# A new hand-made issue order for the last four fifths of an attention and gated convolution kernel

## The chip, the cores and the metric

The program runs on one core of one Trainium2 chip. The metric is device time in microseconds (us) of one execution; lower is better. The core's engines are TensorE (PE, with its weight loads shown as PEld), VectorE (DVE), ScalarE (ACT), GpSimd (POOL) and SyncE (SP). SP computes nothing here: it is the queue from which every DMA is issued, one after the other.

## What is computed

Packed attention and then a gated feed-forward block, for 8 batch elements, 8 heads, 576 tokens, head size 64:

```python
p_packed = sm_attn(p, k, v)           # 32 packed queries attend to the 576 tokens
out = sm_attn(q, p_packed, p_packed)  # the 576 tokens attend to the 32 packed rows
x = out, heads side by side           # (8, 576, 512)
h = np.maximum(x @ w_in, 0.0)         # 512 -> 1024
conv_out[s] = sum over k of conv_w[k] * h[s + k - 1]     # three taps along the tokens
gate = 1.0 / (1.0 + np.exp(-conv_out))
return (h * gate) @ w_out             # 1024 -> 512
```

## The kernel before

The work is cut into 271 streams, each a Python generator of steps. A step is one or a few instructions on one engine. The table `ORDER` is a string of two-digit numbers in base 36; each number names a stream, and the program issues that stream's next step. So the table fixes, for each engine, the order in which its instructions are issued, and each engine takes them strictly in that order. Semaphores between the engines are put in by the framework where data or a buffer demands it; the order alone decides how long somebody stands at one. All 1525 steps are in the table.

```python
flow.run([int(ORDER[i : i + 2], 36) for i in range(0, len(ORDER), 2)])
```

`Flow` also carries planned times, but they decide one thing only: how many idle matmuls are put in on PE (`fill`) until the first output matmul has been issued. That happens before step 331.

The streams that matter here, with g a group of four heads of one batch element (16 groups), b a batch element, j one of 8 blocks of 128 hidden features, m one of 36 blocks of 128 output rows:

- **load_kq(g, k or q)**, L405 from group 4 on: four DMAs issued by SP. There are three buffers (`kq`) for all keys and queries, so a load waits until an earlier `head_transpose` has read its buffer.
- **head_transpose(g, k or q)**, L417: one DVE transposition, which gives that buffer back.
- **attention(g)**: scores on PE (L450), row maximum on DVE (L495), exponential on ACT (L499). From group 10 on the 128 x 576 result is transposed by DVE (L507 and L509) and its blocks are put in place by **16 DMAs on SP** (L515, the "moves" below) into the one buffer `a1T`; before group 10 PE does this. Then comes the product P times V on PE (L535, step 5 of the stream), which reads all of `a1T`. A scaling on ACT, a transposition on PE, the second scores on PE (L450), and a softmax of nine DVE and two ACT steps (L559 to L589) follow.
- **packed_weight(b, half)**: PE (L609), a copy on ACT, and the low part on DVE (L632).
- **ffn1(b, j)**: 12 matmuls (L661), then ACT and DVE in turn up to L689.
- **ffn2(m)**: a cast on ACT (L700), a difference on DVE (L703), eight PE steps of three matmuls each (L752), a copy on ACT (L760) and the store, a DMA on SP (L762).

The moves as they stand in the code:

```python
yield Step("SP", 1100, take=["a1T"], give=["ad"], parts=4 * HG)
...
for q in range(4):
    for h in range(HG):
        nc.sync.dma_start(
            out=a1T[32 * q : 32 * q + 32, h].rearrange("r s n -> r (s n)"),
            in_=moved[32 * h : 32 * h + 32, q].rearrange("r s n -> r (s n)"),
        )
```

Of the kernel before, what the change touches and what calls it, by code (L numbers as in the profile page):

```python
# [23 lines left out]
    "060u3r3z0h3w0e3u0u0e463z0q0u0m0e0w060e460v0n0e46170p0m3z0e0m0e0m0u463x3x0u3z0m0m3x143v0m170v3v0m3v48494a48494849"  # L24
    "400t4a48470t47493z0x0m174a48494910474a490u4a12483z474a4b120u0u0t0m48124b1f4b0u120t124c0m4a13184c1f1f4c414b1a1341"
    "1a4c0m4b414d1a4d4b4g1242124c4b1a0u4g4g0u121a4e41126e4d4c4g4341411n4e430u6e0u0m4c0m1b6e4f1n0u6e1c1g1i4h1544431n0m"
    "4f430u1d1i1b4d1a1i430u1a4f450y1k3o290m0u454h4d1a4d1a6e0u1i1i4h45454e6e1i454f0u4f4d0u430u4f4e4f4i4h4e454j11124i4e"
    "4e1j1j4j7e4i1v127e4k1i6f6e4i1o6e1v6e6e4k4k1v234j1q4i6f6e4k4i1q6f6f7f6f1q4i1l1i4l1q6f7f6f6f1r4j6g6g4j121r4k1i1q16"
    "1s1w3p286e1219236f4l6f4l4k232b7g1q1y121a4k6f1q1q1q121y124m7g4l124l4m2b2b4m4j6f1e1m1t124m1a6g4l6g6g6g6g6g6g4m6h6h"
    "4l4m7h1a4m4j1h6g6g1y4n4n7h4n2j4n1a4o4o4p4o4p4p4o4n4p126h6h6h1y4p4o4n4n6h6h6h6h6h1y4p124o206g1a4p6h4o6i1i1y4q4r4q"  # L30
    "1a126i1a1i1z241a4q6i1z1y6j6i6i6i6i6i6i1y6i6i1a1p1a266j1q1y1a4r2j6j6j6j6j2626266j1i2j6k6j6j6j1u1q1i2g6h2r1i1a2c1q"
    "4r1i4s1x1q264t2e6k4s6j4s2r4t4s6k6k6k4t1q2r2e2z4t1i4t4s2e6l22211i6j6i2o6k6k6k4u6k6k4t4s27276l4t1i1q4u4v4s2k1i2e1q"
    "6k4v4v4v4u4w6l261y4w4v4w4u4w1y4v2m26502650261q2f4u6l6l4w2z6l6l6l6l4u4v1i1q4u4w6l1i501q4w6m2z6l4x4y4x6m4x4z4y4x2m"
    "4x4y4z1q4x4z2m374y1q4y4z4x4z4y4y4z4z6n2w6k2p2e6m6m6m6m6m6m6m6m5253542s2m1y2f6m5252536l6m2e5125266n522e54542u2e6n"
    "6n6n6n6n6n6n6n6o5126545253262e52531y521y54556o546n531y2n261y2n555551546o376o6o6o6o6o6o6o536p1y556p2i2h302u53566o"
    "5556266p6p576p6p342m6p5637556p6p6p1y6q2u6n57562626562a6o566q551y575726562u58576p6q596q6q6q6q586q6q6q58582d2e592m"
    "323f592v5957582v5958575859596r1y5a6q2e2m266r1y5b2e266r6r6r6r6r6r3f322l5a26265a5b6s3f6p2q322e6s332x2u6r6r5c5d2m3c"
    "6r2e5c5d2m5c5d6s322e6s385c332e2m2u2m6t6t5d5b3a2u5d2m2e2u5d2u3a6s6s6s3a5d5e5e356q5c6s6s6s2m2y6r322e6s5c5f6t6t2m5e"
    "5f6s3b5c5f3b2m5e2m5f6t6t6t6t6t2t5e2m5f5e5e2e5f6t5f3a3g6t2e6u6u5g5g5g5h5i5h5i5i5k5k32322u3i6v5g2m5g5k5g5h2e5g5i5h"
    "6u6u6u6u6u6u326u6u5j6u5j5j2m6v313i2m5i5i322u3i2m366t3a5j5h5j5j6v6v5h6v6v6v6v6v6v325l2u5j5h5i3a32325l6w5m5n6v6w5m"  # L40
    "5m3a6u6w6x5n2u5m5m5m2u6w6w6w6w6w3a3a6w5l6x5n39326w6w6y5o6x6x6x6v3e3d6x6x6x6x6x3i6y3j32325n5o5o5o5o5o5m2u6x5p6z5o"
    "2u2u32325n6w2u2u5n5p5p5n5p3i6y5p5q6y6y5q5q5q5p5r6y6y6y6y5q5q2u5p5r5r5q6x6z2u5s6y6y6y5t5s5s3j5r325r5s5s6z6z6z6z6z"
    "6z6z6z5r5t5t5t5s5r5t5s5t5t703a3i5u325v326z3a707070707070705v3a323a713a3h5u3i70703i703i3a5u715w7271726z705w3i5w5w"
    "3i5x5x5x3i3a3i5x5x5x5w3a3a5w71717171717171713i3a3i5y3i5v3a5y5y735y72727272725y5y5y72725w3a725z5x3i71605z733i3i5z"
    "72726173737373737373735z5z3i615z606061743i5z60606062746073637461616263637374636361626262646564747474747474646361"
    "6262637575666674667667757575757575757566676567666667756667657467766768697676767676767676777577696968686868687669"
    "696a7868786a69696a6a6a6a77776a6b6c77776d6b6b6c6c6b6b6b6b777777776c6d6d6c6d6d776c6c786d6d797878787878787876787877"
    "7979797979797979797a797a7b7b7a7a7a7a7a7a7a7a7b7b7b7b7b7b7b7b7c7a7a7c7d7b7b797d7c7c7c7c7c7c7c7c7d7c7c7d7d7d7d7d7d"
    "7d7d7d7i7i7d7d7d7d7d7d7d7d"
)  # L50


# [768 lines left out]
```

## Time and profile before

| | |
|---|---|
| median of 3 runs | 405.0 us (404.56 to 406.21) |
| the profiled execution, its own time | 402.9 us |
| its span, first to last instruction | 401.1 us |
| PE busy | 394.1 us (98%) |
| PE weight loads busy | 316.2 us (79%) |
| DVE busy | 341.4 us (85%) |
| ACT busy | 276.3 us (69%) |
| DMA traffic | 49.19 MB, 123 GB/s on average |

A matmul's record overlaps the next one's, so the distance between starts is what a matmul costs, not its record's length. Step 331 of the table is the ffn1 step that lies near 75 us: all that PE, DVE, ACT and SP do up to there is the same in both tables.

### The profile page before, as it was taken

Reading aid. Unit: us, or ns where it says so; the run is one execution under the profiler, and the core shown is the slowest. Engines: PE = TensorE matmul, PEld = TensorE weight load, DVE = VectorE, ACT = ScalarE, POOL = GpSimd, SP = SyncE. Lnnn points to the kernel's source line nnn. Section 1 sums busy time; section 2 is a strip of 40 time slices with the busy share of each in tenths; the row PEclk is TensorE's granted clock in tenths of the full one; section 3 lists DMA queues with packets and bytes.
Section 4 is the critical chain, followed back from the end, with each engine's and each line's share of the span. In section 5 each row is a group of like instructions: output and inputs, shape, how many; then the busy total and the mean of one; then the engine's idle time right before and its main releaser. Section 6 shows DMA issues by size and latency. Waiting matters only on the chain.

```text
span 401.1 us, 8199 instructions
## 1 busy us (share of the span) xinstructions
PE 394.1 (98%) x3297; PEld 316.2 (79%) x3297; DVE 341.4 (85%) x494; ACT 276.3 (69%) x475; POOL 0.9 (0%) x12
## 2 busy tenths in 40 slices
PE   7999999999999999999999999999999999999996
PEld 6667666777968878888877877889678878898886
DVE  0699999999999999999999999999889976786220
ACT  4899999976856787766674685766766576576221
POOL 0000000000000000000000000000000000000000
PEclk9999999999999999999999999999999999999999
DMA  8989998997728771554446551621010000000121
GB/s 289 399 305 274 248 257 231 214 185 132 159 48 155 174 156 49 94 125 94 105 107 136 121 99 58 136 88 37 28 55 26 28 26 28 26 26 2 52 81 52
DMA packets 140378, 49.19 MB, mean 123 GB/s; under 512 B 121244, under 2 KB 132788, under 8 KB 140340
## 3 DMA queue, kind: packets, MB, share of 16 engines
q1 hardware_dynamic: 140340, 48.67, 48.2%
q8 instruction: 26, 0.43, 0.4%
q14 instruction: 12, 0.10, 0.1%
HBM read 37.25 MB, written 9.44 MB: 116 GB/s over the span
## 4 chain that ended last, share of the span: by engine, by line
PE 78%; ACT 7%; SPq 7%; DMA 4%; DVE 1%; issue 1%; ACTq 0%
PE fo L752 41%; PE big L661 20%; PE sm L752 5%; PE big L450 4%; SPq L515 3%; SPq L405 3%; PE big L609 3%; PE sm L535 2%; PE big L434 2%; DMA v<-in_v_dram 1%; DMA out_dram<-o 1%; PE big L525 1%; DMA hgt<-in_k_dram 1%; DMA a1T<-stage 1%; ACT hgt L265 1%
## 5 line engine op out<-in xcount | busy, mean ns | idle before, releaser
L752 PE MATMUL fo<-wo_hi,xhi 128*128 128x512 f32 (+1 forms) x264 | 106.1, 402 | 0.0
L752 PE MATMUL fo<-wo_hi,xlo 128*128 128x512 f32 (+1 forms) x264 | 103.3, 391 | 0.0
L752 PE MATMUL fo<-wo_lo,xhi 128*128 128x512 f32 (+1 forms) x264 | 103.0, 390 | 0.0
L687 ACT ACTIVATE hgt<-hgt 128x576 f32<-128x576 f32 x64 | 43.9, 693 | 26.2 <-DVE hgt L683 25.7
L752 PEld LDWEIGHTS fo<-wo_hi,xhi 128*128 128x128 f32 x264 | 49.9, 189 | 14.3 <-issue 2.4
L679 DVE SCALAR_TENSOR_TENSOR hgt<-hbuf,cw,hgt 128x576 f32<-128x576 f32 x64 | 51.4, 808 | 10.3 <-ACT hgt L677 9.8
L703 DVE TENSOR_TENSOR xlo<-hgt,xhi 128x1024 fp32r<-128x1024 f32 (+1 forms) x44 | 44.5, 1017 | 18.4 <-ACT xhi L700 18.2
L752 PEld LDWEIGHTS fo<-wo_hi,xlo 128*128 128x128 f32 x264 | 49.6, 188 | 12.0
L673 ACT ACTIVATE hbuf<-big 128x576 f32<-128x576 f32 x64 | 41.7, 655 | 23.3 <-PE big L661 22.8
L752 PEld LDWEIGHTS fo<-wo_lo,xhi 128*128 128x128 f32 x264 | 49.6, 188 | 9.2
L661 PE MATMUL big<-a2hi,ghi 128*128 128x288 f32 x256 | 55.5, 298 | 0.0
L661 PE MATMUL big<-a2hi,glo 128*128 128x288 f32 x256 | 54.3, 294 | 0.0
L661 PE MATMUL big<-a2lo,ghi 128*128 128x288 f32 x256 | 54.2, 293 | 0.0
L683 DVE SCALAR_TENSOR_TENSOR hgt<-hbuf,cw,hgt 128x576 f32<-128x576 f32 x64 | 51.0, 804 | 0.7
L677 ACT ACTIVATE hgt<-hbuf,cw 128x576 f32<-128x576 f32 x64 | 49.7, 783 | 1.2
L689 DVE SCALAR_TENSOR_TENSOR hgt<-hgt,hbuf 128x576 f32<-128x576 f32 x64 | 47.1, 749 | 3.3 <-ACT hgt L687 2.8
L700 ACT CAST xhi<-hgt 128x1024 fp32r<-128x1024 f32 (+1 forms) x44 | 39.0, 890 | 12.7 <-DVE hgt L689 4.7
L661 PEld LDWEIGHTS big<-a2hi,ghi 128*128 128x128 f32 x256 | 42.4, 188 | 5.6 <-issue 0.9
L661 PEld LDWEIGHTS big<-a2lo,ghi 128*128 128x128 f32 x256 | 40.9, 188 | 0.0
L661 PEld LDWEIGHTS big<-a2hi,glo 128*128 128x128 f32 x256 | 40.8, 188 | 0.0
L760 ACT COPY o<-fo 128x512 f32<-128x512 f32 (+1 forms) x33 | 19.0, 577 | 28.0 <-PE fo L752 27.5
L495 DVE TENSOR_REDUCE nm<-big 128x1 f32<-128x576 f32 x16 | 11.8, 740 | 11.4 <-PE big L450 11.4
(91 smaller groups left out, 505.4 us busy)
## 6 DMA issues: line engine op xcount, KB each, us to landing
out_dram<-o SPq DMA_DIRECT2D x35, 256.0 KB, 2.2
v<-in_v_dram SPq DMA_DIRECT2D x16, 512.0 KB, 5.1
k<-in_k_dram SPq DMA_DIRECT2D x48, 144.0 KB, 3.3
q<-in_q_dram SPq DMA_DIRECT2D x48, 144.0 KB, 3.3
hgt<-in_moe_w_in_dram SPq DMA_DIRECT2D x3, 1024.0 KB, 8.8
hgt<-in_moe_w_out_dram SPq DMA_DIRECT2D x3, 1024.0 KB, 7.8
a1T<-stage SPq DMA_DIRECT2D x96, 20.0 KB, 1.8
hgt<-in_k_dram SPq DMA_DIRECT2D x2, 576.0 KB, 5.0
```

What stands on the lines that cost most here:

```text
L450: nc.tensor.matmul(out=o.rearrange("c (j r) -> c j r", r=NR) if by_block(g) else o, lhsT=lhs[r, 32 * i : 32 * i + 32], rhs=rhs[r, :, h, :] ...
L661: nc.tensor.matmul(out=t[:, hf, :SH], lhsT=w[:, gg, js], rhs=x[:, hf * SH : (hf + 1) * SH], start=n == 0, stop=n == 3 * NG - 1,)
L673: nc.scalar.activation(out=h[:, 1 : S + 1].rearrange("c (f s) -> c f s", f=2), in_=t[:, :, :SH], func=AF.Relu, scale=0.5)
L677: nc.scalar.activation(out=d, in_=h[:, 1 : S + 1], func=AF.Copy, scale=cw[:, NJ + j : NJ + j + 1])
L679: nc.vector.scalar_tensor_tensor(out=d, in0=h[:, 0:S], scalar=cw[:, j : j + 1], in1=d, op0=ALU.mult, op1=ALU.add)
L683: nc.vector.scalar_tensor_tensor(out=d, in0=h[:, 2 : S + 2], scalar=cw[:, 2 * NJ + j : 2 * NJ + j + 1], in1=d, op0=ALU.mult, op1=ALU.add)
L687: nc.scalar.activation(out=d, in_=d, func=AF.Tanh)
L689: nc.vector.scalar_tensor_tensor(out=d, in0=d, scalar=1.0, in1=h[:, 1 : S + 1], op0=ALU.add, op1=ALU.mult)
L700: nc.scalar.copy(out=hi[:, js, o], in_=src[:, js])
L703: nc.vector.tensor_tensor(out=lo[:, js, o], in0=src[:, js], in1=hi[:, js, o].bitcast(F32), op=ALU.subtract)
L752: nc.tensor.matmul(out=t[:, : fs.stop - fs.start], lhsT=x[:, c, :], rhs=w[:, c, fs], start=c + i == 0, stop=c == NJ - 1 and i == 2)
L760: nc.scalar.copy(out=o[:, fs], in_=sums_of[m, q][:, : fs.stop - fs.start])
```

## The change

Steps 331 to 1525 of the table stand in another order; the first 330 are the same. Each stream still gets the same number of turns, so that the instructions, their sizes and the buffers' counts are the same. On SP, 50 of its 104 steps stand at another place of its queue; on PE 270 of 491, on DVE 333 of 484, on ACT 284 of 446. The first and the three rows about the middle of the changed stretch:

```diff
@@ -24,29 +24,29 @@
-    "4f430u1d1i1b4d1a1i430u1a4f450y1k3o290m0u454h4d1a4d1a6e0u1i1i4h45454e6e1i454f0u4f4d0u430u4f4e4f4i4h4e454j11124i4e"
...
-    "323f592v5957582v5958575859596r1y5a6q2e2m266r1y5b2e266r6r6r6r6r6r3f322l5a26265a5b6s3f6p2q322e6s332x2u6r6r5c5d2m3c"
-    "6r2e5c5d2m5c5d6s322e6s385c332e2m2u2m6t6t5d5b3a2u5d2m2e2u5d2u3a6s6s6s3a5d5e5e356q5c6s6s6s2m2y6r322e6s5c5f6t6t2m5e"
-    "5f6s3b5c5f3b2m5e2m5f6t6t6t6t6t2t5e2m5f5e5e2e5f6t5f3a3g6t2e6u6u5g5g5g5h5i5h5i5i5k5k32322u3i6v5g2m5g5k5g5h2e5g5i5h"
...
+    "4f430u1d1i1b4d1a1i430u1a4f450y1k3o290m0u454h4d1a4d1a6e0u1i1i4h45454e6e1i454f0u4f4d0u430u4f4e4f4i4h4e11454j4e4i12"
...
+    "6o2w5837373f5b6q6q6q6q6q596r2x6p345a6q2m6q6q6r6q2u5c2u6s6r6r6q2m305c2e5c2u323f6r6r6r6r2v6s6r6r2e2v322l2e3f32336r"
+    "2e5d6s6s6s6s6s6s6s6s2e5d6t2q5d38322e5c5c5c2e2e5d2e2m2u6t5d6s5d332m2u2u6u3a6r5b2e2m5d2m3a2m5c6t2u6t3e6t6t2u3a2e2m"
+    "2m6u6t6t5e6t5e5e5f6t2t5g2e3b5e2m5f5f5e325f6s5k323d2u2m5f6v5g6t5g2m5g5e5e2u6u326u322m5g6v2u6u6u325g5k5g2u6u6u6u6u"
...
```

Read as steps, SP's queue in the stretch around groups 12 and 13 is (k, q, v are loads, "moves" the 16 DMAs of a group, "out" the store of an output block):

```
before: k14, moves 11, out 9, q10, out 10, out 11, q12, v13, moves 12, k15, v14, out 12, q13, out 13, moves 13, out 14, q14, out 15, moves 14
after:  moves 11, out 10, k13, v13, out 11, k14, out 12, q12, moves 12, out 13, q15, moves 13, out 14, v15, v14, out 15, q13, out 16, k15, moves 14
```

In the same stretch, PE before has the product of group 12 (L535) ahead of the last six of the eight steps of ffn2(14), after it behind all eight; the product of group 13 stands behind ffn1(4, 6) before, and after it ahead of ffn1(4, 5) and ffn1(4, 6). DVE has head_transpose(13, k) as its 254th step of the table before and as its 283rd after. Near the end of the attention, PE before has both packed_weight(6, ...) steps ahead of ffn2(22), after it only the first; DVE has the same number of steps ahead of the difference of ffn2(22), with the last softmax step of group 13 in the place of the first of group 14.

## Rows read from the trace of the kernel before

**Rows 1.** The page, parts 1 and 2: engine shares, slices of 10 us, granted clock.

```profile
PE 394.1 (98%) x3297; PEld 316.2 (79%) x3297; DVE 341.4 (85%) x494; ACT 276.3 (69%) x475; POOL 0.9 (0%) x12
...
PE   7999999999999999999999999999999999999996
...
PEclk9999999999999999999999999999999999999999
```

**Rows 2.** Windows: stretch, its length, busy us of PE, PEld, DVE, ACT, POOL.

```profile
75.00:398.00 323.00, 322.69 (x2459) 264.19 (x2457) 280.24 (x395) 208.34 (x346) 0.00 (x0) 1.00 0.39 87
...
75.00:203.00 128.00, 127.96 (x1125) 103.21 (x1123) 127.17 (x190) 91.62 (x166) 0.00 (x0) 1.00 0.63 128
...
370.00:390.00 20.00, 20.00 (x88) 16.08 (x87) 4.91 (x4) 5.95 (x8) 0.00 (x0) 1.00 0.17 63
```

**Rows 3.** Chain of waits in order of time: start us, us, what.

```profile
318.44 5.60 PE fo L752 x24
...
324.04 3.12 PE big L661 x24
```

**Rows 4.** Timeline of the SP queue, 185 to 260 us: start, us, instruction, count.

```profile
186.69 2.78 SPq L405 DMA_DIRECT2D q<-in_q_dram  x4
...
195.94 4.11 SPq L405 DMA_DIRECT2D q<-in_q_dram  x4
...
202.10 11.00 SPq L515 DMA_DIRECT2D a1T<-stage  x16
...
213.20 3.00 SPq L405 DMA_DIRECT2D k<-in_k_dram  x4
...
218.44 4.72 SPq L405 DMA_DIRECT2D q<-in_q_dram  x4
...
223.26 0.67 SPq L762 DMA_DIRECT2D out_dram<-o  x1
...
223.97 10.03 SPq L515 DMA_DIRECT2D a1T<-stage  x16
...
234.73 4.55 SPq L405 DMA_DIRECT2D q<-in_q_dram  x4
...
254.72 3.05 SPq L405 DMA_DIRECT2D q<-in_q_dram  x4
```

**Rows 5.** Chain of waits, 200 to 240 us: the last of sixteen moves.

```profile
233.42 1.78 DMA a1T<-stage
```

**Rows 6.** Timeline of PE around the groups' P-times-V products and at 289 us.

```profile
214.36 0.92 PE L535 MATMUL sm<-v,a1T 128*32 128x64 f32 x36
...
234.74 0.31 PE L535 MATMUL sm<-v,a1T 128*32 128x64 f32 x6
...
235.24 0.82 PE L535 MATMUL sm<-v,a1T 128*32 128x64 f32 x30 [0.19 <-DMA a1T<-stage]
...
289.05 0.66 PE L609 MATMUL big<-w_in_sb,ppT 64*32 64x512 f32 x4
...
290.99 0.50 PE L752 MATMUL fo<-wo_hi,xhi 128*128 128x512 f32 x1
```

**Rows 7.** Timeline of DVE at 203 and at 290 us.

```profile
202.91 0.75 DVE L589 TENSOR_TENSOR a2lo<-a2t,a2hi 128x576 fp32r<-128x576 f32 x1
...
289.66 1.25 DVE L703 TENSOR_TENSOR xlo<-hgt,xhi 128x512 fp32r<-128x512 f32 x2
```

**Rows 8.** Groups by line, DVE: count | busy us, mean ns of one | idle.

```profile
L417 DVE STREAM_TRANSPOSE kT<-k 128x1152 f32<-128x1152 f32 x12 | 16.4, 1364 | 0.0
...
L632 DVE TENSOR_TENSOR glo<-big,ghi 128x1024 fp32r<-128x1024 f32 x12 | 14.5, 1208 | 0.0
...
L583 DVE STREAM_TRANSPOSE a2t<-s 128x576 f32<-128x576 f32 x16 | 12.2, 763 | 0.1
...
L589 DVE TENSOR_TENSOR a2lo<-a2t,a2hi 128x576 fp32r<-128x576 f32 x16 | 11.9, 745 | 0.1
...
L507 DVE STREAM_TRANSPOSE stage<-a 128x512 f32<-128x512 f32 x6 | 6.5, 1092 | 0.0
```

More of the change, by code (lines that the diff above doesn't have):

```diff
@@ L26 @@
     "1a4c0m4b414d1a4d4b4g1242124c4b1a0u4g4g0u121a4e41126e4d4c4g4341411n4e430u6e0u0m4c0m1b6e4f1n0u6e1c1g1i4h1544431n0m"
-    "4f430u1d1i1b4d1a1i430u1a4f450y1k3o290m0u454h4d1a4d1a6e0u1i1i4h45454e6e1i454f0u4f4d0u430u4f4e4f4i4h4e454j11124i4e"
-    "4e1j1j4j7e4i1v127e4k1i6f6e4i1o6e1v6e6e4k4k1v234j1q4i6f6e4k4i1q6f6f7f6f1q4i1l1i4l1q6f7f6f6f1r4j6g6g4j121r4k1i1q16"
-    "1s1w3p286e1219236f4l6f4l4k232b7g1q1y121a4k6f1q1q1q121y124m7g4l124l4m2b2b4m4j6f1e1m1t124m1a6g4l6g6g6g6g6g6g4m6h6h"
-    "4l4m7h1a4m4j1h6g6g1y4n4n7h4n2j4n1a4o4o4p4o4p4p4o4n4p126h6h6h1y4p4o4n4n6h6h6h6h6h1y4p124o206g1a4p6h4o6i1i1y4q4r4q"
@@ L31 @@
[L31 to L35, printed above, removed]
@@ L36 @@
-    "5556266p6p576p6p342m6p5637556p6p6p1y6q2u6n57562626562a6o566q551y575726562u58576p6q596q6q6q6q586q6q6q58582d2e592m"
-    "323f592v5957582v5958575859596r1y5a6q2e2m266r1y5b2e266r6r6r6r6r6r3f322l5a26265a5b6s3f6p2q322e6s332x2u6r6r5c5d2m3c"
-    "6r2e5c5d2m5c5d6s322e6s385c332e2m2u2m6t6t5d5b3a2u5d2m2e2u5d2u3a6s6s6s3a5d5e5e356q5c6s6s6s2m2y6r322e6s5c5f6t6t2m5e"
-    "5f6s3b5c5f3b2m5e2m5f6t6t6t6t6t2t5e2m5f5e5e2e5f6t5f3a3g6t2e6u6u5g5g5g5h5i5h5i5i5k5k32322u3i6v5g2m5g5k5g5h2e5g5i5h"
-    "6u6u6u6u6u6u326u6u5j6u5j5j2m6v313i2m5i5i322u3i2m366t3a5j5h5j5j6v6v5h6v6v6v6v6v6v325l2u5j5h5i3a32325l6w5m5n6v6w5m"
@@ L41 @@
[L41 to L49, printed above, removed]
+    "4f430u1d1i1b4d1a1i430u1a4f450y1k3o290m0u454h4d1a4d1a6e0u1i1i4h45454e6e1i454f0u4f4d0u430u4f4e4f4i4h4e11454j4e4i12"
@@ new lines @@
+    "4j4e1j4i1o7e7e4k4i4j1j6f1v4i1q6e1i6e1i4k1q6e126e4i1i1q1q1v4i6f124j1r4k6e3p161v231l7f4k4j1s4l6e127f201r6f234j4l12"
+    "6g232b4l1q194j4k4k6f6f6f6f4l6f6f6f6f6g4m4m7g121w4m6g1q7g6h1q1a1y6g2b6g4l2b2j4l126h4m1y4k124m1q7h7h1a4m1y124m4l6g"
+    "6g6g6g6g1a4n4o4n4n6g4o1y244n124p4o4o1a4o1q1y4p4p1a4o4p1e4n4n4p4o4n4p4p6i12281h6i6g1t6f6h6h6h6h6h6h6h261y6h4q6h1i"
+    "1a1z1a4q1z1y6i6i6i6j1a1i121a6i2j266i6i6i2j261a1m1a1y266i4q1a2c1i6j4s4t6i4s262r214s4t1y1i4t6h6k1i6j1u1p6j6i2o2e1q"
+    "2r6j6j6j6j4s276j6j2e2r2z4u2e1q4t6j1i4s4s6k1q1i6l2f4u2e2f1q4t4t1i1x4t1i6l6k6k6k6k6k1q6k6k4s276k4v4u4u1q1i4v4u1q4v"
@@ new lines @@
+    "6k6m26262g6j222p4r501y4v2k1q26261y4u4r1y4v1i4v506l6l6l6l6l6l6l6l4r4u6l4w4x4v6m1y1q1i4w4w4w1q4y4x6m6m1y6k4x6m6m6m"
+    "6m4y2a4y4w6l2e4x4x4w4y1q4x4w4x4y4y1q504y4z6m6m4z4z524z1y4z25536m52524z4z522m2e536n2e26261y6n512e54512e536o2z542z"
+    "262m1y6n52526n6n6n6n6n6n6n6m1y26522m552i2h3726532n546n266o2m55532n546o6o6o6o6o6o6o26536p551y516o1y6n262m5355546o"
+    "6p551y265656566p6p6p56546q6p6p6p6p55265626565554562d26572s6p57576p58595858576q5758592m2m5959585a59572u5a5b585759"
+    "6o2w5837373f5b6q6q6q6q6q596r2x6p345a6q2m6q6q6r6q2u5c2u6s6r6r6q2m305c2e5c2u323f6r6r6r6r2v6s6r6r2e2v322l2e3f32336r"
@@ new lines @@
+    "2e5d6s6s6s6s6s6s6s6s2e5d6t2q5d38322e5c5c5c2e2e5d2e2m2u6t5d6s5d332m2u2u6u3a6r5b2e2m5d2m3a2m5c6t2u6t3e6t6t2u3a2e2m"
+    "2m6u6t6t5e6t5e5e5f6t2t5g2e3b5e2m5f5f5e325f6s5k323d2u2m5f6v5g6t5g2m5g5e5e2u6u326u322m5g6v2u6u6u325g5k5g2u6u6u6u6u"
+    "6u5f2u3a5k5h5h5h5f5h2u3b5h2u2m6v6v5i355i5i6v6t2y6u3c5i5i5h3a5j5j5j5h5i5j5i5j5j6v6v6v6v3g5j6v315m5n5o5m6w6w5n5n32"
+    "5n2u5m325m325n325l5o6v3a3i3i2u5l5o6x3a5n325n322u6x5m5o323i3j5o6w6w6w6w3a6w6w6w6w6w5p6x6x6x6x6x6x6x5m5m5l6x6v6y5p"
+    "5p5p6y2u5o3i6x5q366w2u5p326y6y6y6y6y6y6y326z5q326y5p5q5q39325p3j5q5o6z325r5s6y5q6z5q5r5r5t5r5r5s5s3a5s5r5s5t5r5t"
@@ new lines @@
+    "5t5t5s5s5t5t6x70703i6z6z6z6z6z6z6z3i3a5u6z3i3i6y70707070707070703i3h3a3a3a715u3a713a3a3a6z3i5v703i3a5v3i3a3i5u3a"
+    "3i703i72723a71717171717171715w3i3i3i713i735w5w5w3i5w5w3i5w7272727272735x5x5x5x72727271725y7373735x5v5z745y5x5y74"
+    "5x5y5y6073737373735z5y5z5z5z5y606061605z735z60606061616274637462616162626261617273636363626263646465646563637575"
+    "74747474747474666666657467766766667575666675757575676775676768756968676875766876767676767768686969776a6a69696969"
+    "767676776a766a68786a6b6a756a786b6b6b6b776c776c6c6b6c6c6c6c77776b6d6d7777777878787878766d6d6d776d6d79797878787979"
@@ L50 @@
+    "797977787a787a7979797979797a7a7a7a7a7a7a7a7b7b7c7a7a7c7b7b7b7b7b7b7b7b7c7c7c7c7b7d7d7c7c7b7c7c7d7d7d7d7d7d7d7d7c"
+    "7c7d7d7d7d7d7i7i7d7d7d7d7d"
 )
```

## Prediction

> **What bounds the kernel now.** The page comes first: PE is busy for 394.1 of 401.1 us, every slice but the first and the last reads 9, and the granted clock is full all along, 2.4 GHz [rows 1]. A record of a matmul overlaps the next, so a busy share of 98% does not yet say that PE is full. The chain of waits does: 24 output matmuls stand in 5.60 us and 24 of ffn1 in 3.12 us [rows 3], that is 0.700 us for an ffn2 step of three and 1.56 us for an ffn1 step of twelve, one behind the other without a gap. From the changed step on, 36 blocks of eight ffn2 steps and 64 blocks of ffn1, less what is done by then, have to pass at that pace whatever their order, and the windows show PE busy for 322.69 of the 323 us from 75 to 398 [rows 2]. So an order can win only what PE loses in short waits, and it can lose as much as it likes.
>
> The windows also show a second full engine: DVE is busy for 127.17 of the 128 us from 75 to 203 [rows 2]. Where both are full, a step of DVE cannot start earlier than the work ahead of it in DVE's list allows, and a step of PE not earlier than PE's list allows. That gives a way to read a new order against an old trace: take a step, list what stands ahead of it on its engine in either table, and move its old time by the difference. Third, SP: from 202 to 250 us its queue issues almost without a pause, a group of 16 moves taking 10.03 to 11.00 us and a load of q or k 2.78 to 4.72 us [rows 4]. The one place in the stretch where PE visibly stands still for a DMA is there: the product of group 13 starts at 234.74 us, does 6 of its matmuls and goes on at 235.24 [rows 6], when the last move, issued at 233.42, has landed 1.78 us later [rows 5].
>
> **The change part by part.** Nothing is removed or added, and the idle matmuls are all issued ahead of the changed step, so their number stays.
>
> *PE's own work.* The same matmuls cost the same. Counting the table, PE goes 16 times instead of 15 from full to 32-column matmuls and back. The first full matmul after such a group has a record of 0.50 us [rows 6] against a spacing of 0.233 (5.60 / 24); I bound the pair by 0 and 0.3 us and take 0.1.
>
> *The moves of group 12.* In the new table SP issues q12 right ahead of moves 12 (before, q12 went out at 195.94 and a load of v stood between). q12 needs a kq buffer, and the first one given back is that of head_transpose(13, k). When does DVE reach that? Take the moment 202.91 [rows 7]. Of what the new table puts ahead of head_transpose(13, k), DVE before has still to do four steps: two L589, one L583, one L632, 2 x 0.745 + 0.763 + 1.208 = 3.46 us [rows 8]. In return it has by then done work that the new table puts behind: a transposition of k (1.364), the moves' transposition L507 (1.092) with its small companion L509, and three more steps of 0.1 to 0.75 us; together about 3.5 us, from which L417 and L507 are read and the rest is estimated by L589. The two cancel: head_transpose(13, k) starts near 202.8 and ends near 204.2. Then q12: six loads of this kind in the rows take 2.78, 4.11, 3.00, 4.72, 4.55 and 3.05 us [rows 4], 3.70 on average; SP is free at 207.9. From the first move to the last are 9.45 us (223.97 to 233.42) and the last lands 1.78 us later: 219.1 us. With the quickest and the slowest load, and 0.97 us more for the slowest group of moves, the landing lies between 218.2 and 221.1.
>
> When does PE want them? The steps ahead of the product of group 12 are those of before plus six ffn2 steps: 214.36 [rows 6] + 6 x 0.700 = 218.56. So PE waits 0.6 us (0 to 2.5).
>
> *The moves of group 13.* SP goes on at 207.9 + 10.1 = 218.0, the store of block 13 takes 0.67 [rows 4], then the new table has q15, again 3.70: moves 13 begin near 222.4 and have landed 11.23 us later, at 233.6. With all terms at their lowest it is 231.7, with all at their highest 237.7. PE arrives early: ahead of this product the new table has exactly the steps of before less ffn1(4, 5) and ffn1(4, 6), so 234.74 - 2 x 1.56 = 231.6. PE is 2.0 us behind (0.1 to 6.1) after this wait; the wait for group 12 lies inside that figure. Nothing covers it: behind the product PE's queue holds the second scores of group 12 and all of ffn2(16), and an engine takes its list in order. From here PE is full to the end [rows 2], so that the delay is kept. Taken off is what before loses at the same product, about 0.4 us (235.24 less the end of six matmuls at their pace). Net +1.6 us.
>
> *ffn2(22).* Ahead of its difference (L703) DVE has as many steps as before, one exchanged for another of its length, so it comes at 289.66 and ends at 290.91 as before [rows 7]; PE's first step followed at 290.99. In the new table packed_weight(6, second half) is behind it, half of the 1.94 us from 289.05 to 290.99 [rows 6]: PE would be there 1.0 us earlier and wait 1.0 us. If PE comes 1.6 to 2.0 us late from groups 12 and 13 the wait is gone: I count 0, with 1.0 as its bound. Read the other way it is a floor: even if the moves are all in time, DVE holds PE here for about 1 us, unless DVE saves some of the 0.83 us that it idles from 75 to 203.
>
> *Everything else that is moved.* The other loads, the stores, queries, sums and casts change places too. I cost them at nothing: by the same reading of lists no other load reaches its DVE or PE step later than it is wanted. The cover is buffers, three for kq and two for v; without it one load costs the 2.78 to 4.72 us above. ACT is busy for 208.34 of 323 us [rows 2], so it can catch up what it gets late. The bound for all short waits together is 0 to 1 us on either side.
>
> Sum: 1.6 + 0.1 + 0 = 1.7 us on the profiled execution's 402.9 us, 404.6 us. The median of the runs shown lies 2.1 us above that execution, and I add the change to it: 405.0 + 1.7 = **406.7 us**, 0.4%.
>
> **A page against the rows.** The Trainium skill, "Perfetto Trace Analysis", section "Identifying the Most-Contended Engine", says that a matmul busy share is no measure of headroom and that the share of the weight loads should be read in its place. By that rule PE is full to 264.19 / 323 = 82% [rows 2], and a better order could find 58 us. The rows disagree for this kernel: in a stretch where PE does nothing but ffn2 without a gap, 370 to 390 us, the weight loads are busy for 16.08 of 20 us, 80%. So 80% is what full looks like here, and nothing is left.
>
> **The rivals.** (a) *The same mechanism at its upper prices.* If the two loads take 4.7 us each, as two of the six in the rows did, or DVE is late at 204.2, moves 13 land up to 237.7 us and PE loses up to 6.1 - 0.4 = 5.7 us; the middle of what lies beyond the bound is about 4 us, 409 us. It decides as soon as moves 13 land after 234.0 us, 0.4 us later than I take. For it: moves come right behind a load in both groups. Against it: q12 goes out after a pause of SP, and the two loads behind a pause, at 195.94 and 254.72, took 4.11 and 3.05 us. (b) *DVE sets the end.* The late products delay DVE too, and the 1.0 us at ffn2(22) comes on top: 407.7 us. For it: DVE is as full as PE. Against it: a delay of PE of more than 1.0 us hides that wait, unless DVE is late by as much. (c) *Faster.* The ordinary runs are 2.1 us longer than the profiled one, so they hold waits that the trace does not show; if these are late loads and the new table issues just those earlier, they go, and the time is 405.0 - 2.1 = 402.9 us. Against it: the new table issues k15 and q13 later, not earlier. (d) *The rule on weight loads holds* and PE has room. DVE, full to 203 us, would hold back most of it; I price it at 3 us, a twentieth of what PE's free share would be, 402 us.
>
> **How the numbers follow.** This kernel's runs spread by 0.4%, so I take 0.5% (2.0 us) as what can be told from no change. Forecast, a small loss within 0.5%: 0.47, likeliest own range 404.5 to 407.0. (a) 0.34 and (b) 0.07 are slower by more. (c) 0.10 and (d) 0.02 are faster by more. So 0.12 faster, 0.47 same, 0.41 slower. The range goes down to 403.2, leaving out most of (c) and (d), and up to 409.6, which takes in most of (a).
>
> **What would show it.** In the profile after, PE's first long gaps should stand ahead of the L535 matmuls of groups 12 and 13, put down to the moves (DMA a1T), with PE one to three us behind from there on; moves 12 should begin near 208 us and moves 13 near 222. ffn2(22) should start without a wait of 1 us, or with one if the moves were in time. Wrong would be: head_transpose(13, k) well away from 203 us, loads of 3 us both times with PE not waiting at all, or a wait elsewhere, at a PSUM buffer or at a load, that I counted as covered.

## The result and the profile after

The changed kernel takes 407.98 us in the median of its runs against 405.0 of the kernel before beside it, a ratio of 1.0077 (95% interval 1.0052 to 1.0102); one execution of 770.75 us, far off all others, is left out of the ratio. A second comparison, made with the experiments, gives 406.96 against 404.25, 1.0066 (1.0042 to 1.0089). So the change costs 2.7 to 3.0 us, where 1.7 were forecast: inside the range, but past the 0.5% that the likeliest case stood on. The two profiled executions lie further apart than that, 407.98 and 402.9 us.

The page of the changed kernel, engine shares, slices and clock, answers to [rows 1]:

```profile
span 406.0 us, 8189 instructions
...
PE 395.5 (97%) x3297; PEld 317.0 (78%) x3297; DVE 341.7 (84%) x494; ACT 276.5 (68%) x475; POOL 0.9 (0%) x12
...
PE   7999999999999999999999989899999999999996
...
PEclk9999999999999999999999999999999999999999
```

Two slices of PE read 8 now, the 24th and the 26th, that is near 235 and 260 us. The windows of the changed kernel (stretch, its length, busy us of PE, PEld, DVE, ACT, POOL) say how much, and answer to [rows 2]:

```profile
75.00:398.00 323.00, 319.90 (x2424) 260.85 (x2423) 280.90 (x396) 208.48 (x346) 0.00 (x0) 1.00 0.38 86
...
220.00:270.00 50.00, 47.11 (x430) 37.95 (x431) 46.47 (x68) 31.35 (x52) 0.00 (x0) 1.00 0.52 111
...
370.00:390.00 20.00, 20.00 (x88) 16.08 (x87) 6.21 (x7) 6.42 (x9) 0.00 (x0) 1.00 0.14 52
```

and the kernel before in the stretch that matters:

```profile
220.00:270.00 50.00, 49.81 (x397) 40.63 (x396) 48.65 (x71) 33.59 (x55) 0.00 (x0) 1.00 0.45 105
```

From 220 to 270 us the records of PE leave 2.89 us idle, before 0.19; everywhere else from 75 to 398 us they leave 0.2. The waits of the whole span (us in total, times, longest) name one cause that is large, the product of a group (L535) and its moves:

```profile
PE sm L535 <- DMA a1T<-stage: 2.9, 7, 0.9
```

SP's queue in the changed kernel (start, us, instruction, count; answers to [rows 4]):

```profile
204.92 2.71 SPq L405 DMA_DIRECT2D q<-in_q_dram  x4
207.72 11.06 SPq L515 DMA_DIRECT2D a1T<-stage  x16
...
219.50 3.23 SPq L405 DMA_DIRECT2D q<-in_q_dram  x4
222.91 11.33 SPq L515 DMA_DIRECT2D a1T<-stage  x16
...
238.18 6.50 SPq L405 DMA_DIRECT2D q<-in_q_dram  x4
...
245.53 3.14 SPq L405 DMA_DIRECT2D k<-in_k_dram  x4
248.76 11.07 SPq L515 DMA_DIRECT2D a1T<-stage  x16
```

and PE at the products of groups 12, 13 and 14 (answers to [rows 6]; in brackets the idle time ahead and what ended it):

```profile
219.68 0.31 PE L535 MATMUL sm<-v,a1T 128*32 128x64 f32 x6
220.15 0.80 PE L535 MATMUL sm<-v,a1T 128*32 128x64 f32 x30 [0.16 <-DMA a1T<-stage]
...
233.71 0.27 PE L535 MATMUL sm<-v,a1T 128*32 128x64 f32 x2 [0.58 <-DMA a1T<-stage]
234.21 0.30 PE L535 MATMUL sm<-v,a1T 128*32 128x64 f32 x2 [0.23 <-DMA a1T<-stage]
234.84 0.30 PE L535 MATMUL sm<-v,a1T 128*32 128x64 f32 x2 [0.33 <-DMA a1T<-stage]
235.49 0.82 PE L535 MATMUL sm<-v,a1T 128*32 128x64 f32 x30 [0.35 <-DMA a1T<-stage]
...
260.13 0.62 PE L535 MATMUL sm<-v,a1T 128*32 128x64 f32 x6 [0.89 <-DMA a1T<-stage]
261.11 0.82 PE L535 MATMUL sm<-v,a1T 128*32 128x64 f32 x30 [0.36 <-DMA a1T<-stage]
```

At 233 us the product reads its blocks as they land, a pair of matmuls behind each of the last moves, until the sixteenth is there. The chain of waits of the changed kernel goes through the last move of either group (answers to [rows 5]), and ahead of it through the transposition that was to come first, [rows 7], and the load of q behind it:

```profile
203.60 1.29 DVE kT L417
...
233.65 1.80 DMA a1T<-stage
235.49 0.82 PE sm L535 x30
...
259.24 1.83 DMA a1T<-stage
```

The pace of PE is what it was: 24 matmuls of ffn1 stand in 3.12 us as in [rows 3], and the gapless stretch from 370 to 390 us has its weight loads busy for 16.08 of 20 us as in [rows 2].

### The profile page after: what moved, and what is told of

Its sections match the earlier page's. It is cut to its first block, busy times and chain, and to the rows that moved or that the text cites. A ratio compares the mean times of both kernels' runs of the same rounds, so it can differ in the third digit from the quotient of the medians.

```text
span 406.0 us, 8189 instructions
## 1 busy us (share of the span) xinstructions
PE 395.5 (97%) x3297; PEld 317.0 (78%) x3297; DVE 341.7 (84%) x494; ACT 276.5 (68%) x475; POOL 0.9 (0%) x12
## 4 chain that ended last, share of the span: by engine, by line
PE 72%; DVE 10%; DMA 6%; ACT 5%; SPq 5%; issue 1%; DVEq 0%; ACTq 0%
PE fo L752 37%; PE big L661 18%; PE sm L752 5%; SPq L515 4%; PE big L450 3%; DMA stage<-in_moe_w_in_dram 2%; PE sm L535 2%; PE big L609 2%; PE big L328 2%; DMA a1T<-stage 1%; DVE hgt L679 1%; DVE hgt L683 1%; PE big L525 1%; SPq L405 1%; DMA q<-in_q_dram 1%
```

## The experiments

The theory: SP's queue brings the moves of groups 13 and 14 later than PE wants them, and PE, full to the end, keeps what it loses there. The rivals: the new order costs PE time by itself, wherever; or the cost lies in its last third. All ratios are to the kernel before, run on the same chip, which took 404.20, 404.42, 403.60 and 404.25 us in the four lots of runs.

**Half of the table each (two runs).** The seam lies at 196 us.

```diff
-ORDER = old
+ORDER = new[:830] + old without those steps     # e1
+ORDER = old[:830] + new without those steps     # e2
```

> The new table's first 830 steps, up to about 196 us, then all that is left in the old table's order; same instructions. Theory 1 (the loss is made where SP's moves of groups 12 to 14 reach PE late, from 220 us on, and the old order of loads has them in time): at most 1 us over the kernel before, about 405 to 406 us, and PE stands still at the product of group 13 for no more than the 0.4 us of before. Rival 2 (the loss is the sum of many small waits on ACT and DVE all along the changed stretch): about 100 of the 205 us to where PE is full are new, so some 1.2 of 3 us, and more than 1.0 us lost ahead of 196 us.

> The old table's first 830 steps, up to about 196 us, then all that is left in the new table's order, with q12 and q15 right ahead of the moves. Theory 1: most of the loss, 2 to 3 us over before, 407 to 408 us, with PE's waits at the products of groups 13 and 14 as in the new table (2.3 and 1.8 us). Rival 2: about half, 406.5 us, spread out.

Measured: 406.08 us, ratio 1.0039 (1.0018 to 1.0061), and 407.96 us, 1.0083 (1.0056 to 1.0109). New then old loses nothing at the products of 13 and 14, but the seam makes a wait of its own, 1.9 us at a packed weight (L609) near 204 us.

The other half has one of 2.1 us at its seam, comes so much later to the product of 13 that it hardly waits there, and keeps a wait at the product of 14 (0.95 us idle in its trace). Two orders that are each consistent don't fit together at a place where they have done different work, so neither run prices a half.

**A clean seam.** At the 1196th step, near 285 us, the two tables have done the same work but for two steps.

```diff
-ORDER = new
+ORDER = old[:1196] + new without those steps
```

> The old table up to its 1196th step (near 285 us), the new one from there on; the two tables have done the same work there but for two steps, so the seam itself should make no wait. Theory (the loss is made by the moves of groups 13 and 14, all of it ahead of 285 us): the time is that of the kernel before, 404 to 405, ratio 0.998 to 1.002. Rival (something in the last third costs as well: the packed weight of 6, the end on VectorE): each us that it costs shows here, 405 to 407, ratio 1.003 to 1.007.

Measured: 405.44 us, 1.0017 (0.9996 to 1.0038). Most of the loss lies ahead of 285 us; up to 0.4% behind it isn't excluded by this run alone, but its trace shows no wait there of over 0.4 us.

**Load 15,q behind the moves.** In SP's list alone:

```diff
-q12, moves 12, out 13, q15, moves 13, ..., q13, out 16, k15, moves 14, out 17
+q12, moves 12, out 13, moves 13, ..., q13, out 16, k15, moves 14, q15, out 17
```

> The new table with one step moved: the load of q15 (four DMAs) goes behind the moves of group 14 and not ahead of those of group 13. Theory 1: moves 13 begin 3.3 us earlier, near 219.5 us, and moves 14 too; PE's waits at both products go to under 0.5 us, and 3 to 3.5 us come back: the time of the kernel before, 404.5 to 405.5 us. If moves are late for other reasons (the rate of DMA, not the queue), the waits stay and the time is 408 us. Rival 2: no change, 408 us.

Measured: 406.15 us, 1.0033 (1.0015 to 1.0051), about half of the loss given back. The products in this run, PE's timeline:

```profile
233.21 1.03 PE L535 MATMUL sm<-v,a1T 128*32 128x64 f32 x36
...
257.90 0.81 PE L535 MATMUL sm<-v,a1T 128*32 128x64 f32 x6 [0.75 <-DMA a1T<-stage]
259.06 0.80 PE L535 MATMUL sm<-v,a1T 128*32 128x64 f32 x30 [0.35 <-DMA a1T<-stage]
```

The 36 matmuls of group 13 stand without a gap, so the load in front of its moves was what made it late. Group 14 still waits: its moves stand behind 13,q and 15,k, which this edit leaves in place. The expected full return was wrong; there were two late groups, not one.

**The moves on two queues (four runs).** The table untouched, half of the 16 moves issued by POOL, for all groups in the changed kernel, for all groups in the kernel before, and in the changed kernel for group 13 or 14 alone:

```diff
-                    nc.sync.dma_start(
+                    (nc.sync if q < 2 else nc.gpsimd).dma_start(                 # all groups
+                    (nc.gpsimd if g == 13 and q >= 2 else nc.sync).dma_start(    # one group
```

> The changed kernel with half of each group's 16 moves (those with q of 2 and 3) issued by POOL instead of SP; the order table is untouched. No trace shows POOL issuing such DMAs; if it issues one in about the 0.69 us that SP takes, eight last 5.5 us instead of 11 and land 5 us sooner. Theory (SP's queue lands the moves of 13 and 14 late): the waits at the products of 12, 13 and 14 are gone, 4.5 us in the profile, and the time falls to 403.5 to 405, ratio to the kernel before 0.998 to 1.002. Rival (the new order costs PE its time by itself: switches, late VectorE work, and the waits at the products only stand where other waits would): the waits go but the time stays above 406.5, ratio over 1.005.

> The kernel before with half of each group's 16 moves issued by POOL, as in the run beside it. Before loses some 0.6 us at the products of the moved groups. Theory (the queue only costs where it lands late): 403.4 to 404.2, ratio 0.998 to 1.000, and the gap between this run and the changed kernel with two queues is within 1 us. Rival (two queues help by themselves, whatever the table): a gain of over 2 us here too, and the gap of 3 us between the tables stays.

> The changed kernel with half of the moves of group 13 alone issued by POOL (8 of 16, about 0.49 us each there by the run with all groups so). They land some 5 us sooner, so the product of 13 waits for nothing (2.5 us back), and SP is free 5 us sooner after them, which may take load 13,q and with it the moves of 14 ahead: in the run with all groups on two queues SP reached the moves of 14 at 245.0, and 11 us of them and 1.8 of landing end at 257.8, against PE at about 257.2. Theory (each group's product costs what its moves are late, and a queue that is freed at 13 serves 14 too): 404.5 to 405.7, ratio 1.000 to 1.003, with under 1 us of wait at the product of 14. Rival (the two lots are separate, as when only load 15,q was put back): 406 to 406.5, ratio 1.003 to 1.005, with 2 us of wait at 14.

> The changed kernel with half of the moves of group 14 alone issued by POOL. Those of 13 land late as in the changed kernel, so 2.5 us are lost at the product of 13; those of 14 land some 5 us sooner, and the 2.0 us at its product are gone. Theory (the lots add up): 405.7 to 406.5, ratio 1.003 to 1.0055. Rival (the wait at 14 only stands for slack that is lost anyway, as another wait follows behind it): 407.2 to 408, ratio over 1.0065, with the 2 us at a later line of PE.

Measured: changed kernel, all groups 404.08 us, 0.9990 (0.9966 to 1.0014); kernel before, all groups 403.99 us, 0.9999 (0.9980 to 1.0018). The theory held in both runs: the loss is gone where the moves land in time, and the kernel before, whose moves are nearly in time, gets nothing. The table itself costs nothing that these runs, with intervals of 0.2% to either side, can tell. POOL's timeline in the changed kernel, and PE's at the three products:

```profile
221.77 3.91 POOL L515 DMA_DIRECT2D a1T<-stage  x8 [10.68 <-PE sm L535]
```

```profile
220.28 1.11 PE L535 MATMUL sm<-v,a1T 128*32 128x64 f32 x36
...
233.46 0.84 PE L535 MATMUL sm<-v,a1T 128*32 128x64 f32 x36
...
257.14 0.84 PE L535 MATMUL sm<-v,a1T 128*32 128x64 f32 x36
```

Group 13 alone: 404.36 us, 1.0015 (1.0001 to 1.0030). That gives back nearly the whole loss, although the moves of 14 go out on SP alone. SP's timeline of that run shows why:

```profile
223.31 6.26 SPq L515 DMA_DIRECT2D a1T<-stage  x8
...
237.07 3.40 SPq L405 DMA_DIRECT2D q<-in_q_dram  x4
...
241.85 2.99 SPq L405 DMA_DIRECT2D k<-in_k_dram  x4
245.20 10.07 SPq L515 DMA_DIRECT2D a1T<-stage  x16
```

Eight moves fewer on SP let a load of v out 4.7 us sooner, load 13,q takes 3.40 us of queue instead of 6.50, and the moves of 14 begin at 245.2 instead of 248.8. In between SP stands still. The waits of its queue from 200 to 270 us of this run (us in total, times, longest) say for what, L378 being a load of v and L535 the product:

```profile
SPq L378 <- PE sm L535: 2.9, 1, 2.9
```

Load 14,v needs the buffer that the product of 13 gives back. In all nine profiles in which 14,v stands behind the product of 13, the load goes out 0.05 to 0.07 us after the product's last matmul, so a late product of 13 holds the moves of 14 back as much as it holds PE; what differs is the time from there to the moves of 14, 12.3 us in the changed kernel and 10.8 here. That mending 13 also mends most of 14 is not shown by this pair alone: PE still loses 0.6 us at 14 in this run against 1.9 in the changed kernel, but the changed kernel profiled a second time loses 0.7 there too.

Group 14 alone: 408.01 us, 1.0088 (1.0061 to 1.0115) over six runs, no gain at all, though the wait at 14 is gone from its trace. These six runs spread from 405.92 to 409.18 us, and the profiled one holds something new: behind the wait at 13 the clock falls. Its windows (the column behind POOL's is the granted clock):

```profile
234.00:236.00 2.00, 0.78 (x12) 0.28 (x4) 2.00 (x4) 1.64 (x3) 0.00 (x0) 1.00 0.11 31
236.00:238.00 2.00, 1.57 (x44) 1.24 (x52) 0.75 (x2) 0.00 (x0) 0.00 (x0) 0.73 0.62 176
238.00:240.00 2.00, 2.00 (x23) 0.89 (x4) 0.89 (x2) 0.93 (x2) 0.00 (x0) 0.50 0.92 286
240.00:242.00 2.00, 2.00 (x10) 1.60 (x9) 2.00 (x3) 0.64 (x2) 0.00 (x0) 0.92 0.79 241
```

0.50 is 1.2 GHz. The shortfall from 236 to 242 us is 2.00 x (0.27 + 0.50 + 0.08) = 1.7 us. As a mean over the span such a fall reads 0.996.

**The changed kernel and group 14 alone, once more, side by side.**

> The changed kernel itself, beside the next run on one chip. Of its first 12 runs two had a mean granted clock of 0.996, which is 3.2 us of 405 at half speed, 1.6 us lost. Theory (PE's standing at the product of 13 for 2.5 us lets the clock fall in some executions, and that is a part of the loss): ratio 1.006 to 1.009, with some runs at a clock of 0.995 to 0.997 again. Rival (these clocks were chance): no run below 0.998.

> The changed kernel with half of the moves of group 14 issued by POOL, a second time: six runs of it spread from 405.9 to 409.2, two of them at a clock of 0.996, so that the first comparison told little. Theory (the lot at 14 adds to that at 13; the clock falls at 13 in some executions): the median is 1 to 2 us below that of the changed kernel beside it, and runs at a clock of 0.996 lie 1 to 2 us above the others. Rival (what is won at 14 is lost again behind it): medians within 0.5 us of each other.

Measured: 406.96 us over 10 runs, 1.0066, and 407.41 us over 12, 1.0075 (1.0049 to 1.0101). By mean granted clock of each execution: changed kernel, eight at 0.998 or more with a median of 406.70, two at 0.996 (407.11 and 408.47); group 14 alone, seven with a median of 406.41 and five at 0.996, of 408.54 to 409.40. So the fall of the clock came again, in the second kernel at a price of 2 us and more, and blurs the comparison. Without it 0.3 us are won at 14, less than the least that was expected, and over all runs the medians lie 0.45 us apart the other way, as the rival said; in the profile of the changed kernel taken beside it the wait at 14 was smaller too:

```profile
260.08 1.02 PE L535 MATMUL sm<-v,a1T 128*32 128x64 f32 x32 [0.20 <-DMA a1T<-stage]
```

**Later products.** PE's list, with one copy of ffn2(15) on ACT, SP's and DVE's untouched: other work is put ahead of the two products.

```diff
-packed_weight(5,0), product 13, ..., ffn2(16).2, .3, ..., .4, .5 | packed_weight(5,1), product 14, scores 15, ffn2(18).2 to .6
+packed_weight(5,0), ffn2(16).2 to .5, product 13, ...            | packed_weight(5,1), ffn2(18).2 to .6, product 14, scores 15
```

> The changed kernel with SP's order untouched; on PE alone four steps of ffn2(16) are put ahead of the product of group 13 and five of ffn2(18) ahead of that of group 14 (one copy of ffn2(15) on ACT goes ahead with them, for its buffer). The moves land as late as in the changed kernel, but PE comes 2.8 and 3.5 us later to their products and has work until then. Theory (the loss is PE standing at these two products, 2.5 and 2.0 us): the waits are gone and 404 to 405.5, ratio 0.999 to 1.003. Rival (what is behind the products, the copies of ACT and VectorE's part, is what is late, so that PE waits elsewhere): 406.5 to 408 with the waits at later lines of PE.

Measured: 406.33 us, 1.0041 (1.0022 to 1.0060). About half is back. Both products stand without a gap, but the waits name a new one, and the timeline where:

```profile
PE fo L752 <- ACT o L760: 1.2, 1, 1.2
```

```profile
257.59 0.50 PE L752 MATMUL fo<-wo_hi,xhi 128*128 128x512 f32 x1 [1.15 <-ACT o L760]
```

ffn2(18) comes so early now that the copy of ffn2(17) hasn't emptied their PSUM buffer. Theory and rival are both half right: the standing at the products is what was lost, and the place that one gives PE instead has waits of its own.

**Five more moves in the kernel before.** Ahead of the moves of 13, five DMAs of the same kind (16 KB each where a move has 20) that copy into columns of `stage` that nobody reads:

```diff
+            for e in range(5 if g == 13 else 0):
+                nc.sync.dma_start(
+                    out=stage[:32, 1280 + 128 * e : 1280 + 128 * e + 128],
+                    in_=blocks[:32, 128 * e : 128 * e + 128],
+                )
```

> The kernel before with five more DMAs of the moves' kind on SP, right ahead of the moves of group 13, into columns that nobody reads: 5 x 0.63 = 3.2 us of SP's queue, the price of the q15 load. Theory 1: PE, which already waits 0.4 us at that product, waits 3.2 us more, and the end moves by 2.7 to 3.2 us: 407.7 to 408.2 us. Rival 2 (SP has slack, PE's order sets the time): within 1 us of before.

Measured: 409.51 us, 1.0133 (1.0097 to 1.0169), 5.3 us, where 2.7 to 3.2 were expected. The queue does what it should: SP's timeline and PE's, where L540 is the product (five lines further down in this kernel):

```profile
224.34 3.06 SPq L514 DMA_DIRECT2D stage<-stage  x5
227.45 10.09 SPq L520 DMA_DIRECT2D a1T<-stage  x16
```

```profile
236.88 0.30 PE L540 MATMUL sm<-v,a1T 128*32 128x64 f32 x2 [1.66 <-DMA a1T<-stage]
237.54 0.30 PE L540 MATMUL sm<-v,a1T 128*32 128x64 f32 x2 [0.37 <-DMA a1T<-stage]
238.27 0.27 PE L540 MATMUL sm<-v,a1T 128*32 128x64 f32 x2 [0.43 <-DMA a1T<-stage]
238.87 0.80 PE L540 MATMUL sm<-v,a1T 128*32 128x64 f32 x30 [0.32 <-DMA a1T<-stage]
```

The waits are 1.66 + 0.37 + 0.43 + 0.32 = 2.8 us, and this execution, at full clock, took 406.37 us, 2.2 more than before's median. The other five had a mean clock of 0.992 to 0.996 and took 408.55 to 412.04. The clock is the likeliest home of the excess; where in these five it fell isn't shown, as only the first was profiled.

## Why the prediction was right in kind and short in size

**PE is full, so a wait is kept.** Right, and it can be followed step by step. The changed kernel and the one with all its moves on two queues have the same list on PE, so their two profiles can be laid over each other. From the first changed step to the product of 12 the changed kernel is 0.3 us the quicker one. From the product of 12 to the step behind the product of 13 the changed kernel takes 2.6 us longer, from the first step of ffn2(17) to the step behind the product of 14 it takes 1.9 us longer, and from there on no stretch between two blocks of ffn2 differs by more than 0.1 us: 4.5 us are lost at these products and none of it comes back. The second profile of the changed kernel loses 2.3 + 0.7 = 3.0 us in the same places, so one profile does not fix the size; the medians say 2.7 to 3.0. The 2.7 us of idle time from 220 to 270 us (2.89 less 0.19) are less than the 4.5 of that profile, because the pairs of matmuls between the waits count as busy.

Rival (d), room in PE by the Trainium skill's rule on the weight loads ("Perfetto Trace Analysis", section "Identifying the Most-Contended Engine"), found no support: the table that lands its moves in time is no faster than the kernel before. The prediction's answer to it, that 80% is what full looks like, holds for ffn2 alone. In the kernel before, a gapless stretch of ffn1 has the weight loads busy all the time (columns as in [rows 2]):

```profile
324.04:327.16 3.12, 3.12 (x25) 3.12 (x25) 2.40 (x4) 1.24 (x2) 0.00 (x0) 1.00 0.22 84
```

So the share at which PE is full goes with the shape of its matmuls, and 82% over a mixed stretch says neither full nor free. That section of the Trainium skill names the share of peak arithmetic (MFU) beside the weight loads; the prediction left it out.

**The moves of 12.** head_transpose(13, k) ran from 203.60, 0.8 us after the forecast; load 12,q took 2.71 us instead of 3.70, and so the moves began at 207.72 against 207.9. PE came at 219.7 instead of 218.6 and waited some 0.4 us (219.68 to 220.15, for six matmuls that need 0.1), where 0.6 (0 to 2.5) was said. Reading two lists against one old trace placed these steps within 1.1 us. Of either difference 0.42 us had nothing to do with the lists: PE's first step behind the change, ffn1(1,1), starts at 75.47 us in the changed kernel's profile and at 75.05 in that of before. (Step 331 itself is not that ffn1 step but one of ACT in the old table and of DVE in the new.)

**The moves of 13.** Begun at 222.91 (said: 222.4), load 15,q with 3.23 us (3.70). From the first to the last move are 10.74 us instead of the 9.45 of [rows 4, 5], so that the last landed at 235.45, not 233.6; the group's first move alone stood for 1.84 us. But PE came 1.5 us later as well, at 233.13 (233.71 less 0.58) instead of 231.6: the 0.42 us from ahead of the change, 0.7 us of its own up to the product of 12, and the wait there. The last move was 2.3 us behind PE, against 2.0, less the 0.4 that before loses: the step holds. The loss of the product is that of the four waits shown, 0.58 + 0.23 + 0.33 + 0.35 = 1.5 us, and of the pairs between them, which stand in 0.3 us each what takes a few hundredths in the block of 30 behind. The condition of rival (a), moves later than 234.0, came true, but its 409 us did not in the medians, since it took PE's arrival as fixed.

**The moves of 14: the step that failed.** "By the same reading of lists no other load reaches its DVE or PE step later than it is wanted" costed them at nothing. They landed at 259.24 + 1.83 = 261.07 us, 1.8 us after PE came (260.13 less 0.89 = 259.24). In the list of steps one could see that this place was close: between the moves of 13 and 14 the new table has 15,v, 14,v, 13,q and 15,k, the old one only 14,q. But the reading carried on with its own mean prices would have found them in time. An estimate from before's trace: PE comes at 251.65 (its start of this product before) + 3 x 1.56 for three ffn1 steps more, - 0.65 for the scores of group 15 less, + 1.6 for the delay at 13, that is 257.3. The moves of 13 end at 222.4 + 10.1, three stores take 2.0, two loads of v 2.5 and two loads of k and q 2 x 3.70, so that the moves of 14 begin at 244.4 and have landed at 255.6, 1.7 us ahead of PE; with both loads at 4.72 us and the slowest moves it is 258.6, 1.3 us behind. Both came later, PE at 259.24 and the moves at 261.07. Of the 5.4 us more of the moves 2.8 are load 13,q, which took 6.50 us, outside the 2.78 to 4.72 of [rows 4], and some 1.1 each the two groups of moves, which stood 11.33 and 11.07 us instead of 10.0 to 10.1. So the step put a term at nothing without working it out, and the rows at hand did not hold its real price. What the product of 14 costs PE varies: set against the same steps of the run with all moves on two queues, it is 1.9 us in the first profile and in the run with 15,q behind, and 0.7 in the second profile of the changed kernel; the medians give 0.3 when 14 alone is mended.

**The clock: left out.** In the forecast a wait costs what it lasts. Of the 22 executions of the changed kernel that are compared, four had a mean clock of 0.996, some 1.6 us each, 0.3 us on the mean. That is small here, and by the same sum 1.6 to 3.2 us in five of the six executions with five more moves.

**ffn2(22).** Counted as 0 with a bound of 1.0. In the changed kernel PE comes from other work straight to its first matmul, 1.0 us after the end of the difference at 292.73 + 1.46 = 294.19. Right. DVE's and PE's timeline:

```profile
292.73 1.46 DVE L703 TENSOR_TENSOR xlo<-hgt,xhi 128x512 fp32r<-128x512 f32 x2
```

```profile
295.17 0.48 PE L752 MATMUL fo<-wo_hi,xhi 128*128 128x512 f32 x1
```

The floor that the prediction reads out of it, 1 us of waiting here if the moves are all in time, did not show: with all moves on two queues the difference ends at 290.33 us, PE comes at 291.31, 1.0 us behind it again, and PE has no wait there. So rival (b), whose 407.7 us lie nearest to the measured time, is out by its mechanism: that number is met by luck.

**PE's own work.** Said 0.1 us. From its first step behind the change to the product of 12 PE takes 144.21 us in the changed kernel, where the lists give 139.31 + 6 x 0.700 = 143.51 from before: 0.7 us more. In the other profiles whose table is the new one up to there it is 144.19 to 144.51, and two others with the old table give 143.8 and 143.9 by the same sum, so the new order costs 0.3 to 1.0 us in small pieces ahead of the first late moves. With the moves on two queues the two kernels come out even all the same (404.08 and 403.99 us). What makes the small pieces was not tried.

No version that beats both kernels came up: the two with two queues lie within the interval of the kernel before.

## What to carry to other kernels

When a hand-made order moves loads on an in-order DMA queue, work out the landing of every group of transfers behind the moved ones, until the queue has been empty once, not only of the first that is late; do it with the slowest loads on record and not with their mean, and follow the buffers that a load waits for, since a late product can hold up the queue through them. Where one queue is full and transfers of one group are wanted together, try a second queue: half of one group on POOL brought back nearly all that the new order lost (1.0015, 1.0001 to 1.0030), a better place in the first queue about half (1.0033, 1.0015 to 1.0051); the intervals overlap, so which is better isn't settled. And price a stall of a full TensorE at more than its length: the kernels that stood for some 2 us and more at the product of 13 or at a seam had a lower clock in a third of their executions here.

## What the hardware showed that was not expected

- **A stall of some 2 us can be followed by a lower clock.** In the changed kernel, the kernel with five more moves, the two halves with a stall of 2 us at the seam, and the kernel with group 14 alone mended, 21 of 64 executions had a mean granted clock of 0.992 to 0.996. In the others (15,q behind, two queues for all or for 13, later products, the clean seam) none of 72 was below 0.998, nor any of 96 executions of the kernel before, run beside them, below 0.999. Two of the 21 were profiled; in the one whose windows are shown the clock stood at 1.2 GHz for about 3 us right behind the wait at the product. In the other, old then new, it fell right behind the 2.1 us at the seam, to 0.91, 0.50 and 0.73 in the three windows from 206 us on, and not behind the wait at 14. Of these three the middle one (columns as above):

```profile
208.00:210.00 2.00, 2.00 (x6) 1.35 (x5) 0.87 (x1) 1.36 (x2) 0.00 (x0) 0.50 1.06 194
```

The length of the stall alone does not decide it: the run with 15,q behind loses 1.9 us at the product of 14 and had no such execution in 12, and the profiled execution with five more moves stood for 2.8 us and kept its clock. The Trainium skill, "TensorE: Matmul & The Clock Gate", section "HAM oscillation — how this bites in real kernels", tells of a matmul kernel that waits for its DMAs and then starts at the lower clock. The trace agrees, with a difference: here it happens in some executions only, and the wait is broken by pairs of matmuls.
- **A load's time on the queue goes with how closely two loads of v stand ahead of it.** Load 13,q took 6.50, 5.63, 5.03, 5.32, 5.23 and 5.24 us of SP's queue where 15,v had begun 3.3 to 3.7 us before it, and 3.36 to 3.40 us where it had begun 4.9 to 9.5 us before (later products, two queues for all and for 13). That the nearness is the cause was not tried.
- **POOL issues these small DMAs faster than SP** (20 KB each): eight in 3.91 us, 0.49 each, against 5.0 to 6.2 us for eight on SP in the same run. Their landing is slower, as the issues of that run show (KB each, median us to landing):

```profile
a1T<-stage POOLq DMA_DIRECT2D x32, 20.0 KB, 2.4
a1T<-stage SPq DMA_DIRECT2D x32, 20.0 KB, 1.9
```

The Trainium skill, "DMA: Bandwidth & Descriptors", section "Issuing engine by pattern", calls the path of the sync engine generally the faster one; the landing times agree, the issue times here do not.
